# Attention with a local window beside it: score matmuls that ride along, PV in joint bursts, full-width projections

## The chip, the cores and the metric

The kernel runs on one core of a Trainium2 chip. Its engines are TensorE (PE in the profile: matmuls, and PEld, their weight loads), VectorE (DVE), ScalarE (ACT: exp), GpSimd (POOL) and SyncE (SP: it starts transfers). They run side by side, each through its own list of instructions in order, and wait for one another by semaphores. The metric is the device time of one execution in microseconds. Before the change it is 983.29 us (median of 3 runs, 983.21 to 985.47). The execution with a profile spans 983.9 us.

## What is computed

Two attention blocks read the same x (2048 tokens, 512 columns, bf16), and a gate per token mixes them:

```python
def reference(A_x, A_wqkv, A_wo, B_x, B_wqkv, B_wo, gate_w):
    ...
    x = A_x
    g = _sigmoid((x * gate_w).sum(-1, keepdims=True))
    a = _A_ref(x, A_wqkv, A_wo)      # 32 heads of 16, softmax over all 2048 keys
    b = _B_ref(x, B_wqkv, B_wo)      # 32 heads of 16, softmax over 8 keys, 2 apart, backwards
    return g * a + (1 - g) * b
```

Block A is the large one: 32 heads x 2048 x 2048 scores, each of which needs an exp. Block B needs projections on TensorE, and its products and sums run on GpSimd.

## The kernel before

A's work is cut into 32 *periods*: a chunk of 512 queries (`c_`) times a group of 4 heads (`i`). The 4 heads of a group lie on 4 strips of 32 partitions. A *unit* is one head `j` and one block of 128 keys `t`: a score matmul (32 rows x 128 columns of weights, 512 queries) into PSUM, an exp, and a PV matmul into `acc`. A period has 64 units. Most go to ScalarE, in sets of three and two units by turns (PSUM rings `rA` and `rB`); the others go to VectorE, which makes the exp from a polynomial in four operations.

The order of every engine's instructions is fixed when the kernel is built. A small planner runs generators against a model of durations; each `yield (engine, priority, duration, function)` places one step, and the function emits the instructions. `acq` and `rel` take and give back a buffer. Nothing of the planner runs on the chip.

```python
class Plan:
    LAT = 0.08
    ...
P.resource("w", 2)            # two PSUM work banks: projections, transposes, VectorE's scores
P.resource("rA", 1)
P.resource("rB", 1)
P.resource("pTA", 2)
P.resource("pTB", 2)
P.resource("pd", 4)           # results of VectorE's exps
MM = 0.29
```

Projections go through this helper, as four matmuls with 32 columns of weights each, side by side:

```python
def mm_ct(out_, lhsT, rhs, start, stop, **kw):
    for c4 in range(4):
        mm(out_[32 * c4:32 * c4 + 32], lhsT[:, 32 * c4:32 * c4 + 32], rhs, start, stop,
           tile_position=(0, 32 * c4), **kw)

def k_job(i, sc, rel, prio):
    ...
    def pe(c0):
        def f():
            for c in (c0, c0 + 1):
                mm_ct(pk, wkp[:, c, i]..., xT[:, c, sc * QW:(sc + 1) * QW], c == 0, c == DC - 1)
        return f
    yield ("pe", prio, 2 * MM - 0.06, pe(0))
    yield ("pe", prio, 2 * MM - 0.06, pe(2))
```

The same two halves stand in the q projection, in B's projections (`b_proj`, `b_attn`) and, in pairs, in the output projection (`final_job`).

Scores and PV:

```python
def qk_mm(out_, p, t, j):
    c_, i = periods[p]
    mm(out_, kt_all[32 * j:32 * j + 32, i, t * 128:(t + 1) * 128], qt_tiles[p][32 * j:32 * j + 32, :],
       True, True, tile_position=(32 * j, 0))

def pv_step(p, items):
    ...
        for t, j, pt in items:
            pv_left[p] -= 1
            mm(acc[32 * j:32 * j + DH + 1, :], vp_all[:, t, 4 * i + j, :], pt, False, pv_left[p] < 4,
               tile_position=(0, 32 * j))

def pv_job(p, items, res, prio):
    yield ("wait", ev_acc[p])
    ...
    yield ("pe", prio, MM - 0.06 + 0.03 * len(items), pv_step(p, items))

def act_stream():                     # ScalarE's sets
    while front[0] < NP:
        ...
        want = 3 if k % 2 == 0 else 2
        ...                           # units in the order t, j
        yield ("pe", 0, MM - 0.06 + 0.03 * len(units), f)          # f: their scores into the ring
        yield ("spawn", act_tail(k, parts, rname, slot, ring, units))   # exp, then a pv_job

def dve_stream(z):                    # two of these: VectorE's units
    while front[0] < NP - 1 or len(pend[NP - 1]) >= DV_MIN:
        s = yield ("acq", "w", EXP_PRIO)
        ...
        yield ("pe", 1.5, MM - 0.03, lambda: qk_mm(wv_[:], p, t, j))
        ...                           # four VectorE operations, the last into pd
        yield ("spawn", pv_job(p, [(t, j, st["pd"][:])], ("pd", ds), 0.9))
```

So every set's PV is a step of its own, and every VectorE unit has a score step and a PV step of its own. At the end of a period `acc` is copied, transposed (fp32, four matmuls) and divided; after a chunk's last period come the output projections.

Of the kernel before, what the change touches and what calls it, by code (L numbers as in the profile page):

```python
# [47 lines left out]
class Plan:  # L48
# [3 lines left out]
    LAT = 0.08  # L52
# [8 lines left out]

    def resource(self, name, n):
        self.slots[name] = [(0.0, k) for k in range(n)]
        self.reqs[name] = []

# [3 lines left out]
    def advance(self, gen, t, val):  # L69
        while True:  # L70
# [10 lines left out]
            if op == "rel":  # L81
                self.slots[req[1]].append((t, req[2]))
                continue
# [23 lines left out]
            eng, prio, dur, fn = req  # L107
            self.seq += 1
            self.ready[eng].append((prio, self.seq, t, gen, dur, fn))
            return  # L110

    def run(self):
        while True:
            best = None
            for e, lst in self.ready.items():
                if lst:
                    st = max(self.free[e], min(x[2] for x in lst))
                    if best is None or st < best[0]:
                        best = (st, 1, e)
# [9 lines left out]
            if kind == 0:  # L129
                lst = self.reqs[nm]  # L130
                x = min(y for y in lst if y[2] <= st + 1e-9)
                lst.remove(x)
                s = min(y for y in self.slots[nm] if y[0] <= st + 1e-9)
                self.slots[nm].remove(s)
                self.advance(x[3], st, s[1])
            else:
                lst = self.ready[nm]
                x = min((y for y in lst if y[2] <= st + 1e-9), key=lambda y: (y[0], y[1]))
                lst.remove(x)
                x[5]()  # L140
                self.free[nm] = st + x[4]
                self.advance(x[3], st + x[4] + self.LAT, None)


@with_exitstack
def kernel(
# [55 lines left out]

    def mm_ct(out_, lhsT, rhs, start, stop, **kw):
        for c4 in range(4):
            mm(out_[32 * c4:32 * c4 + 32], lhsT[:, 32 * c4:32 * c4 + 32], rhs, start, stop,
               tile_position=(0, 32 * c4), **kw)
# [76 lines left out]
    P.resource("pd", 4)  # L283
    P.resource("prod", 1)
    P.resource("vsh", 1)
    P.resource("ob", 1)
    MM = 0.29
    VP = 0.66
    EXP_PRIO = 60

# [25 lines left out]
    def k_job(i, sc, rel, prio):  # L316
# [3 lines left out]
        s = yield ("acq", "w", prio)  # L320
        pk = wtile(s, [128, QW])

        def pe(c0):
            def f():
                for c in (c0, c0 + 1):
                    mm_ct(pk, wkp[:, c, i].rearrange("p j d -> p (j d)"), xT[:, c, sc * QW:(sc + 1) * QW],
                          c == 0, c == DC - 1)
            return f
        yield ("pe", prio, 2 * MM - 0.06, pe(0))
        yield ("pe", prio, 2 * MM - 0.06, pe(2))  # L330
        kt = kt_all[:, i, sc * QW:(sc + 1) * QW]
        yield ("dve", prio, VP, lambda: V.tensor_scalar(out=kt, in0=pk[:], scalar1=kbias[:, 0:1], scalar2=None,
                                                        op0=ALU.add))
        yield ("rel", "w", s)
# [14 lines left out]
    def v_job(h0, h1, tb, TB, rel, prio):  # L349
# [5 lines left out]
        s = yield ("acq", "w", prio)  # L355
        pv = wtile(s, [128, TB, n])

        def pe(t0, t1):
            def f():
                for tt in range(t0, t1):  # L360
                    for c in range(DC):
                        mm(pv[:, tt, :], xT[:, c, (tb + tt) * 128:(tb + tt + 1) * 128],
                           wv[:, c, h0 * DH:h1 * DH], c == 0, c == DC - 1)
            return f
        step = max(1, TB // 4)
        for t0 in range(0, TB, step):
            yield ("pe", prio, 0.07 * 4 * step, pe(t0, t0 + step))
        yield ("dve", prio, VP, lambda: V.tensor_copy(out=vp_all[:, tb:tb + TB, h0:h1, 0:DH],
                                                      in_=pv[:].rearrange("p t (h d) -> p t h d", d=DH)))
        yield ("rel", "w", s)  # L370
# [6 lines left out]
    def q_job(p, rel, prio):  # L377
# [4 lines left out]
        s = yield ("acq", "w", prio)  # L382
        p1 = wtile(s, [128, QW])

        def pe(c0):
            def f():
                for c in (c0, c0 + 1):
                    mm_ct(p1, wqp[:, c, i].rearrange("p j d -> p (j d)"), xT[:, c, c_ * QW:(c_ + 1) * QW],
                          c == 0, c == DC - 1)
            return f  # L390
        yield ("pe", prio, 2 * MM - 0.06, pe(0))
        yield ("pe", prio, 2 * MM - 0.06, pe(2))
        st = {}

        def absq():
            st["a"] = work.tile([128, QW], BF16, name="absq", tag="absq", bufs=1)
            hi = p1[:].bitcast(I16).rearrange("p (n two) -> p n two", two=2)[:, :, 1]
# [3 lines left out]
        yield ("pe", prio, MM, lambda: mm_ct(p1, selk_all[:, i, :], st["a"][:], False, True,  # L401
                                                skip_group_check=True))

        def evac():
            qt = work.tile([128, QW], BF16, name="qt", tag="qt", bufs=3)
            V.tensor_scalar(out=qt[:], in0=p1[:], scalar1=QSC, scalar2=qbias[:, 0:1], op0=ALU.mult, op1=ALU.add)
            qt_tiles[p] = qt
        yield ("dve", prio, VP, evac)
        yield ("rel", "w", s)
        yield ("set", ev_q[p])  # L410

    def g_job(prio):
# [3 lines left out]
        s = yield ("acq", "w", prio)  # L416
        zp = wtile(s, [128, NT])

        def pe(t0):
            def f():  # L420
                for t in range(t0, t0 + 4):
                    for c in range(DC):
                        mm(zp[:, t:t + 1], xT[:, c, t * 128:(t + 1) * 128], gw[:, c:c + 1], c == 0, c == DC - 1)
            return f
        for t0 in range(0, NT, 4):
            yield ("pe", prio, 0.8, pe(t0))
        e1 = work.tile([128, NT], FP32, name="e1", tag="e1", bufs=1)
        yield ("act", -1, 0.3, lambda: A.activation(out=e1[:], in_=zp[:], func=ACT.Exp, scale=-1.0))
        yield ("rel", "w", s)
# [7 lines left out]
    pend = [deque((t, j) for t in range(NT) for j in range(4)) for _ in range(NP)]  # L437
    front = [0]
    acc_tiles = {}
    pv_left = [64] * NP  # L440
    nset = [0]
    ndve = [0]

# [5 lines left out]
    def pv_step(p, items):  # L449

        c_, i = periods[p]

        def f():
# [6 lines left out]
            for t, j, pt in items:  # L460
                pv_left[p] -= 1
                mm(acc[32 * j:32 * j + DH + 1, :], vp_all[:, t, 4 * i + j, :], pt, False, pv_left[p] < 4,
                   tile_position=(0, 32 * j))
        return f

    def after_pv(p):
        if pv_left[p] == 0:
            return post_job(p)
        return None

    def pv_job(p, items, res, prio):
        i = periods[p][1]
        yield ("wait", ev_acc[p])
        for t, j, _ in items:
            yield ("wait", ev_v[(i, t)])
        yield ("pe", prio, MM - 0.06 + 0.03 * len(items), pv_step(p, items))
        if res is not None:
            yield ("rel", res[0], res[1])
        nx = after_pv(p)
        if nx is not None:  # L480
            yield ("spawn", nx)

    def act_tail(k, parts, rname, rslot, ring, units):
        pname = "pTA" if k % 2 == 0 else "pTB"
        pslot = yield ("acq", pname, k)
        n = len(units)
# [10 lines left out]
        for q_, (p, us) in enumerate(parts):  # L497
            items = [(t, j, pT[:, off + z, :]) for z, (t, j) in enumerate(us)]
            off += len(us)
            last = q_ == len(parts) - 1  # L500
            yield ("spawn", pv_job(p, items, (pname, pslot) if last else None, 1 + 1e-4 * k))

    def act_stream():
        while front[0] < NP:
# [5 lines left out]
            units, parts = [], []  # L510
            p = front[0]
            while want and p < NP:
                us = []
                while want and pend[p]:
                    us.append(pend[p].popleft())
                    want -= 1
# [3 lines left out]
                if not pend[p]:  # L520
# [10 lines left out]
            ring = ps.tile([128, 3 if k % 2 == 0 else 2, QW], FP32, tag=rname, bufs=1, name="ring")  # L531

# [3 lines left out]
            yield ("pe", 0, MM - 0.06 + 0.03 * len(units), f)  # L536
            yield ("spawn", act_tail(k, parts, rname, slot, ring, units))

    DV_MIN = 12

    def dve_pick(t_now):
        p = front[0]
        if p >= NP:
            return None
        if len(pend[p]) >= DV_MIN and ev_q[p].time is not None and ev_q[p].time <= t_now:
            return (p,) + pend[p].pop()
        if p + 1 < NP and len(pend[p + 1]) >= DV_MIN and ev_q[p + 1].time is not None and ev_q[p + 1].time <= t_now:
            return (p + 1,) + pend[p + 1].pop()
        return None

    def dve_stream(z):
        yield ("wait", ev_start[0])
        yield ("delay", 1.0 + 1.5 * z)
        while front[0] < NP - 1 or len(pend[NP - 1]) >= DV_MIN:
            s = yield ("acq", "w", EXP_PRIO)
            t_now = yield ("now",)
            u = dve_pick(t_now)
            if u is None:
                yield ("rel", "w", s)
                yield ("delay", 0.7)  # L560
                continue
            p, t, j = u
            n = ndve[0]
            ndve[0] += 1
            wv_ = wtile(s, [128, QW])
            yield ("pe", 1.5, MM - 0.03, lambda: qk_mm(wv_[:], p, t, j))
            lo = wv_[:].bitcast(U16).rearrange("p (n two) -> p n two", two=2)[:, :, 0]
            ta = work.tile([128, QW], FP32, name="ta", tag="ta", bufs=2)
            pr = 40 + 1e-3 * n
            yield ("dve", pr, VP - 0.05, lambda: V.tensor_scalar(out=ta[:], in0=lo, scalar1=A3, scalar2=None,  # L570
                                                                 op0=ALU.mult))
            yield ("dve", pr, VP - 0.05, lambda: V.scalar_tensor_tensor(out=ta[:], in0=ta[:], scalar=A2, in1=lo,
                                                                        op0=ALU.add, op1=ALU.mult))
            yield ("dve", pr, VP - 0.05, lambda: V.scalar_tensor_tensor(out=ta[:], in0=ta[:], scalar=A1, in1=lo,
                                                                        op0=ALU.add, op1=ALU.mult))
# [403 lines left out]
```

## Time and profile before

| | |
|---|---|
| span of the profiled execution | 983.9 us |
| mean granted TensorE clock | 0.840 |
| TensorE busy, matmuls | 892.3 us, 7296 |
| ScalarE busy | 871.6 us |
| VectorE busy | 677.5 us |
| GpSimd busy | 583.6 us |
| first exp of a set starts, last one ends | 36.46 us, 971.8 us |
| sets of 3, of 2 units, one of 1 | 376, 375, 1 |
| units on VectorE | 169 |

How to read it: nearly all instructions come from one recording line of the kernel (L191), so groups are told apart by the tiles that they write and read. `ring<-qt,kt_all` is a score matmul of a set, `w_...<-qt,kt_all` one for VectorE, `pT<-ring` an exp of a set, `acc<-pT,vp_all` and `acc<-pd,vp_all` are PV. Busy times of matmuls overlap their neighbours', so TensorE's busy share is not its work; the distance from start to start is. The row PEclk gives the clock that TensorE was granted, in tenths, in 40 slices of the span. In the answers by windows, each engine's busy microseconds stand with its number of instructions in brackets, then the clock, the share of the DMA engines, and GB/s.

### The profile page before, as it was taken

Reading aid. Unit: us, or ns where it says so; the run is one execution under the profiler, and the core shown is the slowest. Engines: PE = TensorE matmul, PEld = TensorE weight load, DVE = VectorE, ACT = ScalarE, POOL = GpSimd, SP = SyncE. Lnnn points to the kernel's source line nnn. Section 1 sums busy time; section 2 is a strip of 40 time slices with the busy share of each in tenths; the row PEclk is TensorE's granted clock in tenths of the full one; section 3 lists DMA queues with packets and bytes.
Section 4 is the critical chain, followed back from the end, with each engine's and each line's share of the span. In section 5 each row is a group of like instructions: output and inputs, shape, how many; then the busy total and the mean of one; then the engine's idle time right before and its main releaser. Section 6 shows DMA issues by size and latency. Waiting matters only on the chain.

```text
span 983.9 us, 18122 instructions
## 1 busy us (share of the span) xinstructions
PE 892.3 (91%) x7296; PEld 270.9 (28%) x7296; DVE 677.5 (69%) x1178; ACT 871.6 (89%) x770; POOL 583.6 (59%) x543
## 2 busy tenths in 40 slices
PE   2899999999999988998999989989989989899986
PEld 0333333333232322222223222222223222222221
DVE  3544558576757788875763687888884787987575
ACT  0489999999899998998989998898999988998894
POOL 4000075859989696849786986929974979340000
PEclk8679999999799997798759777796799885976795
DMA  9000103221212103211021411111110201000000
GB/s 249 9 2 1 55 12 98 87 66 25 84 60 79 36 12 97 97 55 51 15 86 36 127 36 51 43 43 44 44 43 12 97 1 44 1 1 1 2 1 22
DMA packets 50021, 47.34 MB, mean 48 GB/s; under 512 B 9984, under 2 KB 47360, under 8 KB 49936
## 3 DMA queue, kind: packets, MB, share of 16 engines
q1 hardware_dynamic: 46240, 41.98, 14.1%
q10 hardware_dynamic: 3696, 4.20, 1.5%
q8 instruction: 57, 0.93, 0.4%
q14 instruction: 28, 0.23, 0.1%
HBM read 37.75 MB, written 6.32 MB: 45 GB/s over the span
## 4 chain that ended last, share of the span: by engine, by line
PE 48%; ACT 24%; DVE 14%; issue 10%; DMA 2%; SPq 0%; ACTq 0%; DVEq 0%
ACT pT L191 24%; PE acc L191 18%; PE ring L191 14%; DVE ta L191 9%; DVE pd L191 3%; DMA xT<-in_A_x_dram 2%; DVE accS L191 1%; ACT lg L191 0%; DVE kt_all L191 0%; DVE lg L191 0%; DVE qt L191 0%; DVE absq L191 0%; PE w_5455 L191 0%; PE w_11876 L191 0%; PE w_6192 L191 0%
## 5 line engine op out<-in xcount | busy, mean ns | idle before, releaser
L191 ACT ACTIVATE pT<-ring 128x1536 bf16<-128x1536 f32 x752 | 867.2, 1275 | 86.4 <-PE ring L191 75.8
L191 PE MATMUL ring<-qt,kt_all 32*128 32x512 bf16 x1879 | 353.4, 436 | 49.2 <-ACT pT L191 43.4
L191 PE MATMUL acc<-pT,vp_all 128*17 128x512 bf16 x1879 | 336.3, 432 | 0.0
L191 POOL TENSOR_TENSOR prod<-prod 128x512 f32<-128x512 f32 (+1 forms) x208 | 240.5, 1170 | 6.3
L191 POOL TENSOR_TENSOR prod<-ksh,qb 128x512 f32<-128x512 bf16 x128 | 144.1, 1157 | 157.1 <-DVE qb L191 114.8
L191 POOL TENSOR_TENSOR prod<-vsh,lg 128x512 f32<-128x512 bf16 x128 | 136.6, 1098 | 117.7 <-issue 114.9
L191 PEld LDWEIGHTS <-kt_all 32*128 32x128 bf16 x2048 | 102.7, 93 | 354.8 <-issue 343.6
L191 PEld LDWEIGHTS <-vp_all 128*17 128x17 bf16 x2048 | 72.4, 89 | 220.9 <-issue 219.4
L191 PE MATMUL acc<-pd,vp_all 128*17 128x512 bf16 x169 | 75.2, 479 | 6.2 <-DVE pd L191 5.4
L191 PEld LDWEIGHTS <-xT 128*32 128x32 bf16 (+1 forms) x1152 | 39.0, 99 | 29.8 <-issue 22.0
L191 DVE COPY accS<-acc 128x512 f32<-128x512 f32 x32 | 22.0, 688 | 14.5 <-PE acc L191 13.7
L191 PEld LDWEIGHTS <-wkp 128*32 128x32 bf16 x512 | 14.4, 103 | 33.8 <-issue 15.4
L191 DVE TENSOR_REDUCE kmax_all<-kt_all 128x1 f32<-128x512 bf16 x32 | 21.8, 684 | 0.9
L191 POOL TENSOR_TENSOR ob<-prod 128x512 f32<-128x512 f32 x16 | 20.3, 1270 | 1.3
L191 POOL TENSOR_TENSOR obb<-ob,prod 128x512 bf16<-128x512 f32 x16 | 20.3, 1270 | 1.3
L191 PEld LDWEIGHTS <-wqp 128*32 128x32 bf16 x512 | 15.9, 107 | 17.7 <-issue 13.8
L191 PE MATMUL acc<-ones_t,z_85 128*32 128x512 bf16 x128 | 15.6, 476 | 2.0 <-DVE accS L191 1.8
L191 POOL TENSOR_TENSOR lg<-prod 128x128 f32<-128x128 f32 x32 | 13.6, 425 | 2.5
L191 PE MATMUL w_136<-xT,wkp 128*32 128x512 bf16 x16 | 2.1, 626 | 11.6 <-DMA xT<-in_A_x_dram 11.6
L191 ACT ACT_TABLE_LOAD x1 | 1.3, 1283 | 12.5 <-DMA xT<-in_A_x_dram 12.5
L191 DVE TENSOR_TENSOR lg<-lg,mx 128x256 f32<-128x256 f32 x16 | 10.9, 680 | 0.2
L191 PEld LDWEIGHTS <-oT 128*32 128x32 bf16 x256 | 8.1, 96 | 6.5 <-issue 2.1
(1286 smaller groups left out, 1127.5 us busy)
## 6 DMA issues: line engine op xcount, KB each, us to landing
ksh<-kv_scr SPq DMA_DIRECT2D x16, 1024.0 KB, 6.2
vsh<-kv_scr SPq DMA_DIRECT2D x16, 1024.0 KB, 5.9
kv_scr<-kvs SPq DMA_DIRECT2D x16, 256.0 KB, 2.3
out_dram<-osb SPq DMA_DIRECT2D x16, 128.0 KB, 1.7
bw<-in_B_wqkv_dram ACTq DMA_DIRECT2D x1, 1536.0 KB, 14.1
wraw<-in_A_wqkv_dram ACTq DMA_DIRECT2D x2, 512.0 KB, 5.8
wv<-in_A_wqkv_dram ACTq DMA_DIRECT2D x1, 512.0 KB, 10.1
bwo<-in_B_wo_dram ACTq DMA_DIRECT2D x1, 512.0 KB, 8.8
```

The source lines that it names most:

```text
L191: return chain_on(self._key, f(*a, **k))
```

## The change

It is meant to give TensorE fewer groups of matmuls for the same work, so that ScalarE gets its scores in time, and to keep TensorE's clock from falling.

- *Riders.* VectorE's units have no stream of their own any more. When a set's two or three scores are placed, a unit of a head whose strip is free in this group may ride along into a work bank (`w`), if a bank and a `pd` buffer are free.
- *PV bursts.* PV of a three-unit set is held until the two-unit set after it is done, and both are issued in one step; finished VectorE units join a burst where their strip has room.
- *Full-width projections.* `mm_ct` is gone; a projection is one matmul of 128 columns of weights per 128 rows of contraction, and its four are one step.
- *Zero-weight matmuls.* If the planner counts less than `WARM` (0.47) of the last 3 us as streaming, a burst gets one more matmul with zero weights, which adds nothing to `acc`.
- *The planner.* New durations (a row `MM` 0.22, a change of group `SW` 0.11); work that isn't scores or PV is placed only when ScalarE has enough sets waiting (`fits`); at most two work banks go to such work; V in smaller pieces and B's tiles start at other times.

The core of the diff:

```diff
-    LAT = 0.08
+    LAT = {"pe": 0.15, "act": 0.08, "dve": 0.08, "pool": 0.08, "sp": 0.08}
+    cap_job = 2
+    refill = 0.56
+    patience = 6.0
 ...
+    def quiet(self, window):
+        while self.streamed and self.streamed[0][0] < self.now - window:
+            self.streamed.popleft()
+        return sum(d - 0.11 for _, d in self.streamed)
 ...
+    def fits(self, x, st):
+        if x[0] < 2 or st - x[7] > self.patience:
+            return True
+        lim = max(self.free["act"], st) + sum(y[4] for y in self.ready["act"]) - self.refill
+        return st + x[4] <= lim or self.free["act"] + 3.0 < st
 ...
-    def mm_ct(out_, lhsT, rhs, start, stop, **kw):
-        for c4 in range(4):
-            mm(out_[32 * c4:32 * c4 + 32], lhsT[:, 32 * c4:32 * c4 + 32], rhs, start, stop,
-               tile_position=(0, 32 * c4), **kw)
 ...
-    MM = 0.29
+    MM = 0.22
+    SW = 0.11
+    WARM = 0.47
 ...
     def k_job(i, sc, rel, prio):
-        yield ("pe", prio, 2 * MM - 0.06, pe(0))
-        yield ("pe", prio, 2 * MM - 0.06, pe(2))
+        def pe(s):
+            w.open(s, [128, QW])
+            for c in range(DC):
+                mm(w.t[:], wkp[:, c, i]..., xT[:, c, sc * QW:(sc + 1) * QW], c == 0, c == DC - 1)
+        yield ("pe", prio, 4 * MM + SW, pe, "w")
 ...
     def pv_job(p, items, res, prio, act=True):
+        if act:
+            act_due[p] -= len(items)
+            if len(items) == 3 and act_due[p] > 0:
+                held_pv[p].append((now, items, res))
+                return
+        def f():
+            ...
+            for h in [h for h in held_pv[p] if h[0] <= now]:
+                todo = list(h[1]) + todo
+            cnt = [sum(1 for x in todo if x[1] == j) for j in range(4)]
+            most = max(cnt)
+            for e in list(pdq[p]):       # finished VectorE units
+                if e[0] <= now and (act_left[p] == 0 or cnt[e[2]] < most) and ...:
+                    todo.append(e[1:4])
+            ...                          # PV of todo, rows by rows
+            if P.quiet(3.0) + MM * max(cnt) < WARM * 3.0 and max(row_left[p]) > 0:
+                mm(acc[32 * j:32 * j + 32, :], z32[:], ones_t[:], False, False, tile_position=(0, 32 * j))
 ...
     def act_stream():
-        yield ("pe", 0, MM - 0.06 + 0.03 * len(units), f)
+        def f():
+            for s_, (p_, t, j) in enumerate(units):
+                qk_mm(ring[:, s_, :], p_, t, j)
+            js = [u[2] for u in units]
+            while len(js) < 4:
+                r = rider(js)
+                if r is None:
+                    break
+                ...
+                qk_mm(wt[:], p_, t, j)
+                P.spawn(dve_unit(p_, t, j, s, ds, wt, ndve[0]), ...)
+        yield ("pe", 0, SW + MM, f)
 ...
-    for z in range(2):
-        P.spawn(dve_stream(z))
-    P.spawn(g_job(20))
+    P.spawn(g_job(4))
 ...
-        P.spawn(b_proj(t, ev_start[min(NP - 1, 1 + 2 * t // 2)] if t else ev_start[1], 25 + 0.1 * t))
-        P.spawn(b_attn(t, ev_start[min(NP - 1, 1 + t)], 25 + 0.1 * t))
+        pr = (9 if t < 2 else 16) + 0.1 * t
+        P.spawn(b_proj(t, ev_start[min(NP - 1, max(1, 2 * t - 3))], pr))
+        P.spawn(b_attn(t, ev_start[min(NP - 1, max(1, 2 * t - 3))], pr))
```

## The prediction

> **What bounds the kernel now.** I read the page first: busy times, the row of granted clock, the chain, the costliest groups.
>
> ```profile
> PE 892.3 (91%) x7296; PEld 270.9 (28%) x7296; DVE 677.5 (69%) x1178; ACT 871.6 (89%) x770; POOL 583.6 (59%) x543
> ...
> PEclk8679999999799997798759777796799885976795
> ...
> ACT pT L191 24%; PE acc L191 18%; PE ring L191 14%; DVE ta L191 9%; DVE pd L191 3%; DMA xT<-in_A_x_dram 2%; DVE accS L191 1%; ACT lg L191 0%; DVE kt_all L191 0%; DVE lg L191 0%; DVE qt L191 0%; DVE absq L191 0%; PE w_5455 L191 0%; PE w_11876 L191 0%; PE w_6192 L191 0%
> ...
> L191 ACT ACTIVATE pT<-ring 128x1536 bf16<-128x1536 f32 x752 | 867.2, 1275 | 86.4 <-PE ring L191 75.8
> ```
>
> ScalarE and TensorE are both near 90%, and 75.8 us of ScalarE's idle time ends with a score matmul (ring). The clock row says when: it is rarely at 9 after the first third. So I asked for the busy times in windows, once over all stretches at half clock from 62 us on and once over all at full clock from 42 us on. First one neighbouring pair, then the two sums.
>
> ```profile
> core 0: us, PE busy (x) PEld busy (x) DVE busy (x) ACT busy (x) POOL busy (x), PEclk, DMA share, GB/s
> 492.26:512.74 20.48, 20.18 (x94) 4.31 (x92) 15.05 (x25) 18.21 (x16) 19.76 (x18) 0.50 0.34 104
> ...
> 512.74:553.70 40.96, 39.34 (x435) 14.19 (x435) 17.08 (x34) 40.35 (x37) 28.77 (x27) 1.00 0.19 58
> ...
> sum 292.26, PE 275.86 PEld 57.00 DVE 210.22 ACT 226.51 POOL 186.92; mean PE 13.14 PEld 2.71 DVE 10.01 ACT 10.79 POOL 8.90
> ...
> sum 651.93, PE 597.17 PEld 205.87 DVE 452.21 ACT 639.99 POOL 385.73; mean PE 28.44 PEld 9.80 DVE 21.53 ACT 30.48 POOL 18.37
> ```
>
> At full clock ScalarE is busy 640 of 652 us (98%): it is the bound. At half clock, 21 stretches and 292 us, it is busy 78% (81% without the tail), while TensorE is at 94% or more: there TensorE is the bound. So the time is ScalarE's work, plus what half clock costs. Next, why the clock falls (windows of 3 us, same columns):
>
> ```profile
> 433.00:436.00 3.00, 2.35 (x17) 0.71 (x16) 2.81 (x6) 3.00 (x3) 3.00 (x4) 1.00 0.55 156
> 436.00:439.00 3.00, 2.47 (x18) 0.75 (x17) 2.82 (x6) 3.00 (x4) 3.00 (x3) 1.00 0.79 255
> 439.00:442.00 3.00, 2.54 (x17) 0.82 (x14) 2.96 (x6) 3.00 (x4) 2.84 (x4) 1.00 0.10 32
> 442.00:445.00 3.00, 2.54 (x15) 0.71 (x14) 3.00 (x6) 3.00 (x3) 3.00 (x3) 0.91 0.00 0
> 445.00:448.00 3.00, 2.57 (x14) 0.44 (x13) 2.08 (x4) 2.09 (x3) 2.92 (x4) 0.50 0.00 0
> ```
>
> Only scores and PV run here, no projection, and after some 12 us of that the clock halves. What a step costs I take from the timeline, full clock at 950 us and half clock at 510 us (start, duration), and ScalarE's pace from a stretch in which it never waited:
>
> ```profile
> 950.12 0.39 PE L191 MATMUL ring<-qt,kt_all 32*128 32x512 bf16 x2
> 950.44 0.60 PE L191 MATMUL acc<-pT,vp_all 128*17 128x512 bf16 x5
> 950.97 0.39 PE L191 MATMUL w_12331<-qt,kt_all 32*128 32x512 bf16 x1
> ...
> 510.34 0.60 PE L191 MATMUL ring<-qt,kt_all 32*128 32x512 bf16 x2
> 510.88 1.02 PE L191 MATMUL acc<-pT,vp_all 128*17 128x512 bf16 x5
> 511.83 1.08 PE L191 MATMUL w_6963<-identf,accS 128*128 128x128 f32 x4
> ...
> 933.83 22.72 ACT L191 ACTIVATE pT<-ring 128x1536 bf16<-128x1536 f32 x20
> ```
>
> Matmuls on different strips of the array run together, so a group costs "rows": the most matmuls that share one strip. A one-row group takes 0.32 us from start to start at full clock, a two-row group 0.53: a row is 0.21 and the change of group 0.11. At half clock they are 0.54 and 0.95: 0.41 to 0.43 and again 0.11. An exp set averages 22.72 / 20 = 1.136 us, a pair (3 and 2 units) 2.27.
>
> **What the Trainium skill says.** "TensorE: Matmul & The Clock Gate", Part 1: the clock is either half or full, by how busy TensorE was in a free-running window of 3413 ns; the trace agrees (0.50 or 1.00 only; stretches such as 13.65 and 20.48 us are multiples of 3.413). Part 3 of that page says matmuls in different strips run together, some 4 ns apart; five PV matmuls in 0.60 us agree. "TensorEngine Tiling", Tiling Modes, Key Properties, says a change of tile shape drains the engine; I read the 0.11 us as that. "TensorE ... Clock Gate", Part 1, "HAM oscillation": gaps between bursts can send the clock back and forth, which is what the windows show.
>
> **The change, part by part.** I counted in the order of instructions of both programs, taking 0.2155 us for a row of 512 columns at full clock (the timeline's 0.21; the Clock Gate page, Part 1, gives 215.7 ns from start to start).
>
> - *Riders.* DVE's score units ride in the free strip of a ScalarE score group. Units for DVE go from 169 to 206, sets from 752 to 737. ScalarE: 15 sets x 1.136 = 17 us less. DVE: 37 x 4 operations at about 0.60 = +89 us, to some 760 us, still under the end.
> - *PV bursts.* PV of a three-unit set waits for the two-unit one. Score and PV rows go from 1740 to 1474, so 266 x 0.2155 = 57 us less TensorE.
> - *Fewer groups.* Changes of tile shape between neighbours go from 1677 to 1204: 473 x 0.11 = 52 us less.
> - *Full-width projections.* Four strips side by side or one full-width matmul are both one row: 608 rows before and after. No stream time is won, only instructions (7296 matmuls to about 5300); a projection now adds a change of shape (in the 1204) and is one block of 4 x 0.21 + 0.11 = 0.97 us, where it was two halves.
> - *Zero-weight matmuls.* 135 against 128: only 7 were placed. They can hardly warm anything.
> - *Head and tail.* First exp at 36.5 us, last end 971.8 of 983.9: 36.5 + 12 = 48.5 us, unchanged.
>
> TensorE at full clock: before 542 us of streams + 1677 x 0.11 = 727; after 485 + 132 = 617. A steady pair at full clock falls to 2 x 0.32 + 0.53 = 1.17 us; at half clock to 2 x 0.54 + 0.95 = 2.03, which now fits into ScalarE's 2.27. Before, it was 4 x 0.54 = 2.16 plus 0.45 DVE units with scores and PV of their own, above 2.27.
>
> The sum. Before: 48.5 + 752 x 1.136 (854) + 8 for the small exps (16 of 0.46 us and one shorter) leaves 73 us lost, 12 of them at full clock, some 61 at half clock. After: 48.5 + 737 x 1.136 (837) + 8 = 893.5, + 13 lost at full clock, + what half clock still costs. That last term is the open one.
>
> It has two factors. How often: fewer rows also means a less busy engine. A bare pair is 4 rows in 2.27 us, 38% streaming, against 46% with DVE units of their own. I gave each set in the two orders ScalarE's measured pace and counted the rows placed between set and set: 33% of the 3.4 us windows stream under 47% in the changed one, 14% before. How dear: without a projection nothing is lost now; a projection at half clock is a block of 4 x 0.43 + 0.11 = 1.8 us, of which the pair's slack (0.24) hides little, so some 1.5 us of exp time. Twelve such blocks would cost 18 us, thirty 45. A block also brings the clock back: before, every stretch ended in a window with a projection or a transpose in it. I take about 16 stretches, fewer than the 21 of before since projections are spread, with one block each: 24 us. Predicted: 893.5 + 13 + 24 = 930 us.
>
> **Rivals.** (1) *The clock stays up*: projections and B's tiles are now spread over the run instead of clumped, and the planner weighs its last 3 us. Then half clock costs under 5 us and the time is about 905. Against it: only 7 zero-weight matmuls, though bare stretches are at 38%. (2) *The clock falls more often*: every bare window drops it, 35 stretches of one and a half blocks, 2.2 us each, 77 us; 893.5 + 13 + 77 is 983, the time of before, and all that riders and bursts won is given back. Half of it, 38 us, makes 945. For it: the 33% against 14%. Against it: the dearest part of the old loss, TensorE too slow in bare stretches, is gone by arithmetic. (3) *DVE becomes the bound*: 760 of 930 us is 82%, and riders hold one of two work banks for four operations, so a projection may wait for a bank with TensorE stopped in order behind it. Before, only 5.4 us of TensorE's idle time ended with a pd; I allow 10 us.
>
> **Range and chances.** 899 (rival 1 and a little less lost) to 964 (57 us at half clock, three quarters of rival 2, or half of it with 3 on top). Faster by over 2% is under 963.6: 0.84. Within 2%: 0.12, rival 2 nearly full. Slower: 0.04, if 2 and 3 both hold in full.
>
> **What would show it.** Right: about 1.136 us per set without waits, 737 sets, ScalarE 98% at full clock and at least 88% at half clock, bare half-clock pairs at ScalarE's pace, its idle time before ring near half of 75.8, head and tail the same. Wrong: a mean clock under 0.8 with ScalarE as idle as before; idle time of TensorE ended by DVE; or ScalarE waiting at full clock.

## The result, and the profile after

The changed kernel takes 948.93 us (median of 4 runs, 937.99 to 952.73), the kernel before 983.25 us: a ratio of 0.961, 95% interval 0.952 to 0.970. Predicted were 930 us and a range of 899 to 964. The ratio leaves out the slowest of the four runs, and the profile is of that one: it spans 951.0 us.

From its page: busy times, the granted clock in 40 slices, the chain of waits, and the exps' group.

```profile
PE 800.1 (84%) x5415; PEld 233.3 (25%) x5415; DVE 762.0 (80%) x1326; ACT 851.9 (90%) x755; POOL 582.7 (61%) x543
...
PEclk9999999979879977778689967768788977876795
...
ACT pT L252 48%; PE w L252 11%; PE ring L252 9%; PE acc L252 7%; DMA xT<-in_A_x_dram 2%; DVE ta L252 2%; DVE pd L252 1%; ACT lg L252 0%; DVE kt_all L252 0%; DVE qt L252 0%; DVE vp_all L252 0%; DVE osb L252 0%; DMA out_dram<-osb 0%; SPq L252 0%; DVE accS L252 0%
...
L252 ACT ACTIVATE pT<-ring 128x1536 bf16<-128x1536 f32 x737 | 847.9, 1289 | 74.9 <-PE w L252 34.3
```

The chain now runs through the exps for 48% of the span (24% before); TensorE's three entries here make 27% (scores and PV alone made 32%, all of TensorE 48%). But the clock row still dips from the first third on, and the idle time in front of the exps fell only from 86.4 to 74.9 us. The windows over all stretches at half clock (first sum) and at full clock (second) say it in numbers:

```profile
sum 302.01, PE 274.29 PEld 55.48 DVE 235.80 ACT 254.12 POOL 163.31; mean PE 11.93 PEld 2.41 DVE 10.25 ACT 11.05 POOL 7.10
...
sum 600.79, PE 497.65 PEld 166.98 DVE 502.40 ACT 584.63 POOL 408.48; mean PE 21.64 PEld 7.26 DVE 21.84 ACT 25.42 POOL 17.76
```

ScalarE is busy 97% at full clock (98% before), and 84% at half clock (78% before), the tail included both times. There is as much half clock as before, some 300 us. What happens in one such stretch is seen in windows of one clock period (3.413 us; busy us and count of PE, PEld, DVE, ACT, POOL, then the clock):

```profile
398.35:401.76 3.41, 2.12 (x20) 0.57 (x15) 3.16 (x6) 3.41 (x5) 3.41 (x4) 1.00 0.01 2
401.76:405.17 3.41, 3.06 (x21) 0.55 (x20) 3.34 (x6) 3.40 (x4) 3.33 (x4) 0.50 0.00 0
...
408.59:412.00 3.41, 3.26 (x18) 0.55 (x15) 3.38 (x6) 3.40 (x4) 3.41 (x4) 0.50 0.00 0
412.00:415.41 3.41, 3.41 (x19) 0.78 (x17) 2.90 (x5) 1.45 (x2) 3.25 (x3) 0.50 0.00 0
```

In the first window only scores and PV run, and the clock falls. In the next ones, at half clock, ScalarE is busy 3.40 of 3.41 us: bare scores and PV cost it nothing now. In the last one it drops to 1.45 us. The timeline shows what ran then:

```profile
411.43 0.61 PE L252 MATMUL ring<-qt,kt_all 32*128 32x512 bf16 x2
411.97 1.89 PE L252 MATMUL w<-xT,wqp 128*128 128x512 bf16 x4
413.79 0.61 PE L252 MATMUL ring<-qt,kt_all 32*128 32x512 bf16 x3
414.33 0.62 PE L252 MATMUL acc<-ones_t,z 128*32 128x512 bf16 x4
414.73 0.94 PE L252 MATMUL acc<-pT,vp_all 128*17 128x512 bf16 x5
...
415.49 1.45 ACT L252 ACTIVATE pT<-ring 128x1536 bf16<-128x1536 f32 x1 [2.04 <-PE acc L252]
```

A full-width projection starts at 411.97 and the next scores only at 413.79, 1.82 us later; ScalarE waits 2.04 us. The projection is not all of it: the scores are done at 414.40, but the wait ends with PV (`PE acc`). A `pT` buffer comes free when PV has read it, and the burst that reads it (414.73) stood behind the projection, the scores and the four matmuls that open the next accumulation. In the window after this one the clock is at full again.

To compare runs I split each span. An exp of three units starts 1.331 us after the one before when nothing waits, one of two units 0.904 us. The work is their sum; whatever lies beyond it from one start to the next is a loss, put down to the clock at the earlier start. Up to the first record of the clock, near 50 us, it counts as half; 1.2 to 5.3 us of the loss at half clock lie before 60 us. At full clock I keep waits over 2.2 us apart. Head and tail are the times before the first and after the last exp. All in us; the last two columns are the stretches at half clock that are not over by 60 us and begin before the last exp ends. One that runs on into the tail is counted whole: 12 us of the 290 are tail, none of e3's 24. Each row is one execution, which can lie some us off the median of its runs.

| run | span | work | head + tail | lost at half clock | lost at full clock, short + long waits | stretches | their us |
|---|---|---|---|---|---|---|---|
| before | 983.9 | 839.9 | 48.6 | 74.3 | 21.0 + 0 | 21 | 290 |
| changed | 951.0 | 823.4 | 47.5 | 59.4 | 16.2 + 4.2 | 23 | 300 |
| e1 no zero rows | 947.0 | 823.4 | 48.6 | 52.4 | 18.2 + 4.3 | 25 | 285 |
| e2 zero rows in parallel | 933.2 | 826.5 | 48.2 | 31.6 | 19.0 + 7.6 | 25 | 157 |
| e4 serial zero rows, some | 929.1 | 824.3 | 46.3 | 27.6 | 20.7 + 9.8 | 19 | 99 |
| e3 serial zero rows, all bursts | 921.6 | 826.5 | 48.2 | 10.2 | 28.8 + 7.6 | 7 | 24 |
| e11 the same, limit 90% | 923.0 | 824.7 | 47.4 | 13.7 | 27.4 + 9.7 | 10 | 44 |
| e5 before, with zero rows | 950.1 | 843.9 | 47.0 | 33.1 | 25.9 + 0 | 10 | 99 |
| e7 projections in strips | 942.5 | 823.4 | 47.8 | 51.8 | 15.3 + 4.2 | 23 | 293 |
| e8 own scores | 950.5 | 824.3 | 48.1 | 41.0 | 20.9 + 16.0 | 22 | 222 |
| e10 own scores, zero rows | 933.0 | 831.0 | 47.0 | 9.7 | 28.0 + 17.1 | 8 | 44 |
| e6 own PV | 998.3 | 828.3 | 47.4 | 90.9 | 18.5 + 13.0 | 38 | 338 |
| e9 own PV, zero rows | 964.4 | 831.0 | 48.0 | 25.2 | 31.9 + 28.0 | 14 | 61 |
| e12 own PV, halved projections | 946.5 | 831.0 | 47.3 | 14.2 | 17.3 + 36.4 | 8 | 38 |

From before to changed: 16.5 us less exp work, 15 us less lost at half clock. That is nearly all of the gain in these two traces.

### The profile page after: what moved, and what is told of

Its sections match the earlier page's. It is cut to its first block, busy times and chain, and to the rows that moved or that the text cites. A ratio compares the mean times of both kernels' runs of the same rounds, so it can differ in the third digit from the quotient of the medians.

```text
span 951.0 us, 14436 instructions
## 1 busy us (share of the span) xinstructions
PE 800.1 (84%) x5415; PEld 233.3 (25%) x5415; DVE 762.0 (80%) x1326; ACT 851.9 (90%) x755; POOL 582.7 (61%) x543
## 4 chain that ended last, share of the span: by engine, by line
ACT 49%; PE 27%; issue 18%; DVE 4%; DMA 2%; SPq 0%; ACTq 0%; DVEq 0%
ACT pT L252 48%; PE w L252 11%; PE ring L252 9%; PE acc L252 7%; DMA xT<-in_A_x_dram 2%; DVE ta L252 2%; DVE pd L252 1%; ACT lg L252 0%; DVE kt_all L252 0%; DVE qt L252 0%; DVE vp_all L252 0%; DVE osb L252 0%; DMA out_dram<-osb 0%; SPq L252 0%; DVE accS L252 0%
## 5 line engine op out<-in xcount | busy, mean ns | idle before, releaser
L252 ACT ACTIVATE pT<-ring 128x1536 bf16<-128x1536 f32 x737 | 847.9, 1289 | 74.9 <-PE w L252 34.3
L252 DVE SCALAR_TENSOR_TENSOR ta<-ta,w 128x512 f32<-128x512 f32 x412 | 278.2, 682 | 6.8
L252 PE MATMUL acc<-pT,vp_all 128*17 128x512 bf16 x1842 | 272.9, 450 | 0.4 <-ACT pT L252 0.2
L252 DVE TENSOR_SCALAR ta<-w 128x512 f32<-128x512 uint16 x206 | 141.4, 687 | 42.2 <-PE w L252 40.0
L252 DVE SCALAR_TENSOR_TENSOR pd<-ta,w 128x512 uint16<-128x512 f32 x206 | 139.8, 680 | 3.1
L252 PE MATMUL w<-qt,kt_all 32*128 32x512 bf16 x206 | 94.0, 458 | 0.0
L252 PEld LDWEIGHTS <-vp_all 128*17 128x17 bf16 x2048 | 46.2, 90 | 113.3 <-issue 111.8
L252 PE MATMUL w<-xT,wkp 128*128 128x512 bf16 x128 | 37.7, 423 | 19.0 <-DMA xT<-in_A_x_dram 17.2
L252 PE MATMUL w<-bw,xT 128*128 128x512 bf16 x192 | 51.4, 392 | 0.5 <-DVE otok L252 0.2
L252 PE MATMUL w<-xT,wqp 128*128 128x512 bf16 x128 | 50.2, 536 | 0.0
L252 PEld LDWEIGHTS <-xT 128*128 128x128 bf16 x512 | 32.7, 103 | 37.0 <-issue 23.8
L252 DVE COPY accS<-acc 128x512 f32<-128x512 f32 x32 | 22.0, 687 | 10.2 <-PE acc L252 10.2
```

What stands on the lines that cost most here:

```text
L252: return chain_on(self._key, f(*a, **k))
```

## The experiments

My theory after the result: the clock falls in every 3.4 us window in which too few rows stream, every projection at half clock makes ScalarE wait, and this is what keeps the gain small. The rivals: extra rows only take TensorE's time, or what counts is the number of matmuls and groups. Ratios are to the kernel before, with 95% intervals.

### Is it the clock? Zero-weight rows, four ways

The change's own zero-weight matmul can do little even where it is placed: it goes to the strip with the most PV left, which mostly has one matmul in a burst where another strip has two. So it mostly runs *beside* the burst's second row and adds no streaming (by the trace 73 of e2's 376 begin a row of their own, and 2 of the change's 7).

**e1**, no such matmul:

```diff
-    WARM = 0.47
+    WARM = 0.0
```

> No zero-weight rows beyond the 128 that open an accumulation; nothing else is changed. Both theories: the 7 rows of the changed kernel did nothing, so 0.96 of the time before, 940 to 955 us, about 300 us at half clock.

Measured: 942.4 us, ratio 0.960 (0.957 to 0.964), 285 us at half clock. The 7 rows did nothing.

**e2**, one in every burst, strip as in the change:

```diff
-    WARM = 0.47
+    WARM = 9.0
```

> One zero-weight matmul in every PV burst (376), in the strip that is furthest behind, which mostly runs beside the burst's own second row: TensorE streams 19 us more, not 81. Theory (the clock falls where a 3.4 us window streams under 45%, and half clock is what the change still loses): such windows fall only from 27% to 18%, so 935 to 948 us and at least 180 us at half clock. Rival A (the clock follows the number of matmuls, not the streamed time): under 100 us at half clock, 915 to 925 us. Rival B (added matmuls only take TensorE's time): over 950 us.

**e3**, the same number in the same bursts, but in a strip that the burst uses most:

```diff
-    WARM = 0.47
+    WARM = 9.0
-                j = max(range(4), key=lambda j_: row_left[p][j_])
+                j = max(range(4), key=lambda j_: (row_left[p][j_] > 0, cnt[j_]))
```

> The same 376 zero-weight matmuls in the same places, each in a strip that the burst uses twice already, so that each adds a row: TensorE streams 79 us more. Theory: windows under 45% fall to 8%, half clock to under 110 us, ScalarE idle 30 us less; it has 3.6 us more work (199 units on VectorE, not 206): 912 to 925 us. Rival A: the same as its neighbour with the rows in parallel. Rival B: 79 us more TensorE makes it slower than the changed kernel, over 955 us.

e2's page, and then e3's: clock, and the group of zero-weight matmuls (both with the 128 that open an accumulation).

```profile
PEclk8599999999989988768999998989898998887895
...
L252 PE MATMUL acc<-ones_t,z 128*32 128x512 bf16 x504 | 165.5, 417 | 1.7 <-DVE accS L252 1.2
```

```profile
PEclk9999999999999999999999999999999999999997
...
L252 PE MATMUL acc<-ones_t,z 128*32 128x512 bf16 x504 | 156.7, 389 | 1.9 <-DVE accS L252 1.6
```

Both have 504 such matmuls and the same lists otherwise. In e2 they lie beside other rows: 935.1 us, 0.952 (0.948 to 0.955), 157 us at half clock. In e3 nearly each is a row of its own (350 of 376 by the trace): 925.6 us, 0.942 (0.939 to 0.945), 24 us at half clock, and the loss at half clock falls from 52 us (e1) to 10. The rival that counts matmuls falls, and so does the one in which added rows only cost: TensorE got 79 us more to stream by the order of instructions (some 75 by the trace's rows) and the kernel became 17 us faster than e1, 0.6 us above the range that I gave. It didn't come for nothing: short waits at full clock rose from 18 to 29 us. e2 came out at the lower end of what I expected, with somewhat less half clock than the 180 us.

**e4**, serial rows only under 62%: the same strip as in e3, with

```diff
-    WARM = 0.47
+    WARM = 0.62
```

> Serial zero-weight rows only where the planner counts under 62% of its last 3 us as streaming: 127 rows, 26 us more streaming, windows under 45% at 15%. Theory: half clock about 180 us, 925 to 938 us, between the changed kernel and the one with a row in every burst. Rival B: 950 to 960 us.

Measured: 930.2 us, 0.947 (0.943 to 0.951), 99 us at half clock, in between as the theory has it, with less half clock than the 180 us that I expected.

**e5**, the kernel before with zero-weight rows and nothing else of the change (the planner counts what streams, and plans 0.22 us for the row):

```diff
+            if len(items) == 3 and pv_left[p] > 8 and P.quiet(3.0) < 0.62 * 3.0:
+                j = items[-1][1]
+                mm(acc[32 * j:32 * j + 32, :], z32[:], ones_t[:], False, False, tile_position=(0, 32 * j))
+                return 0.22
```

> The kernel before, with its own scheduling, groups and projections; alone a serial zero-weight row after a three-unit PV where the planner counts under 62% of its last 3 us as streaming: 138 rows, 27 us more streaming. Windows under 45% fall from 10% to 2.5%; VectorE gets 160 units, not 169, so ScalarE has 4 us more work. Theory: half clock under 120 us (before 290), 925 to 945 us, the clock alone being worth as much as the whole change. Rival (TensorE was simply overloaded, and rows added to it cost): 985 to 1010 us.

```profile
PEclk8679999999999997797999988999999999799977
```

Measured: 949.7 us, 0.961 (0.956 to 0.966): 138 rows of zeros in the old kernel are worth as much as the whole change. Half clock 99 us, the loss there 33 in place of 74. The time is 5 us beyond my range; ScalarE has 4 us more work and loses 5 more at full clock.

### The parts of the change

**e7**, projections in four strips again (`mm_ct` in place of `mm`, for all that fill a bank with 512 columns):

> The changed kernel with its projections as four matmuls of 32 columns of weights side by side again (14 thousand instructions on TensorE's list, not 10.6). Rows are the same, the order is the same. Theory: no difference beyond 1%, 940 to 952 us. Rival (full width is faster, or wakes the clock by using the whole array): over 960 us, or a half-clock time that differs from 300 us by over 60.

```profile
PE 793.6 (84%) x7239; PEld 239.4 (25%) x7239; DVE 761.9 (81%) x1326; ACT 851.2 (90%) x755; POOL 583.4 (62%) x543
```

Measured: 942.9 us, 0.957 (0.953 to 0.961), 293 us at half clock. 1800 more matmuls change nothing that can be told. Full width is neither faster nor does it hold the clock better.

**e8**, VectorE's scores as steps of their own:

```diff
-                while len(js) < 4:
+                while False:
                     r = rider(js)
 ...
+    def dve_stream(z):
+        ...
+        while front[0] < NP - 1 or rem(NP - 1) >= DV_MIN:
+            r = rider([])
+            ...
+            yield ("pe", 1.5, SW + MM, lambda: qk_mm(wt[:], p, t, j))
```

> The changed kernel without riders: a VectorE unit's score is a step of its own again, chosen by the same rule (204 units). The order shows that most such steps still land right beside a score group: 8 us more streams, 13 more changes of group. Theory: within 1% of the changed kernel, 938 to 955 us, possibly less half clock, since windows under 45% go from 27% to 21%. Rival (riders are the gain): 960 us or more.

Measured: 953.0 us, 0.969 (0.966 to 0.973): some 10 us slower than e1 and e7 by the medians, 3.5 by the traces of e1 and e8. It loses 41 us at half clock (e1: 52) but 12 us more in long waits. **e10** adds serial zero-weight rows, so that the clock is out of it:

> VectorE's scores as steps of their own, with a serial zero-weight row in every PV burst. ScalarE has 4.5 us more work than in the run with riders and the same rows (925.6 us). Theory: without riders ScalarE lost 15 us more at full clock and less at half clock; with the clock up only the first is left, so 940 to 950 us. Rival (riders are worth nothing): 928 to 934 us.

Measured: 934.7 us, 0.950 (0.947 to 0.953), 9 us slower than e3. 4.5 us of that are ScalarE's work and 9.5 long waits. Riders are worth about 1%, between what the two theories said.

**e6**, each set's PV at once (without zero rows, to be read beside e1):

```diff
-            if len(items) == 3 and act_due[p] > 0:
+            if False:
                 held_pv[p].append((now, items, res))
```

> The changed kernel without the holding of PV: each set's PV is a group of its own again (no zero-weight rows, to be compared with the run without them). The rows stay nearly as they are (490 us of streams, not 484), the changes of group go from 1206 to 1686, 53 us more TensorE; 195 units on VectorE, so 5 us more ScalarE. Theory (TensorE has room at full clock, and a bare pair at half clock is 2.16 us, under ScalarE's 2.27): 950 to 965 us, of which 5 are ScalarE's. Rival (fewer changes of group are the gain): 980 us or more.

```profile
PEclk8599979799987888868677998657778888887686
...
L252 ACT ACTIVATE pT<-ring 128x1536 bf16<-128x1536 f32 x741 | 850.9, 1257 | 116.8 <-PE ring L252 52.2
```

Measured: 1002.7 us, 1.019 (1.015 to 1.022): 60 us slower than e1, slower than the kernel before, far beyond what I expected and where the rival put it. The rows are nearly as many. By the table, whose two traces are 51 us apart, e6 loses 38 us more than e1 at half clock, at much the same price per stretch (2.4 and 2.1 us), but in 38 stretches in place of 25: the clock comes back sooner, after 8.9 us and not 11.4 on average, and falls again. 9 us more go to long waits and 5 to ScalarE's work. So I held the clock up too, **e9** (zero-weight rows after three-unit PV, serial):

```diff
-    WARM = 0.47
+    WARM = 9.0
 ...
+            if len(items) == 3 and P.quiet(3.0) + MM * max(cnt) < WARM * 3.0 and max(row_left[p]) > 0:
+                j = max(range(4), key=lambda j_: (row_left[p][j_] > 0, cnt[j_]))
```

> PV of each set as a group of its own, and a serial zero-weight row after every three-unit PV (355 rows): 563 us of streams and 1683 changes of group. ScalarE has 4.5 us more work than in the run with held PV and a row in every burst (925.6 us). Theory (the 60 us that own PV groups cost came through the clock, which fell 39 times): windows under 45% are 2%, half clock under 80 us, 930 to 945 us. Rival (the 480 more changes of group delay ScalarE at full clock too): 965 us or more with the clock up.

Measured: 965.5 us, 0.982 (0.978 to 0.985), with only 61 us at half clock. My theory that nearly all of it came through the clock falls: of the 60 us 40 stay against e3, and the time is where the rival put it. By the table 20 of them are long waits at full clock, 15 half clock, 4.5 work and 3 short waits. The longest wait is here (timeline of e9, start and duration):

```profile
99.16 0.39 PE L252 MATMUL ring<-qt,kt_all 32*128 32x512 bf16 x3
...
100.41 1.04 PE L252 MATMUL w<-xT,wkp 128*128 128x512 bf16 x4
...
105.84 4.09 PE L252 MATMUL w<-wv,xT 128*128 128x128 bf16 x64
...
111.75 0.38 PE L252 MATMUL w<-absq,selk_all 128*128 128x512 bf16 x1
...
112.48 0.74 DVE L252 TENSOR_SCALAR qt<-w,qbias 128x512 bf16<-128x512 f32 x1
...
113.59 0.39 PE L252 MATMUL ring<-qt,kt_all 32*128 32x512 bf16 x2
...
114.10 5.80 ACT L252 ACTIVATE pT<-ring 128x1024 bf16<-128x1024 f32 x5 [12.73 <-PE w L252]
```

ScalarE runs out of a head group's units at 99 us, and the next group's k, V and q are only then projected: 12.73 us. A new theory, for the rival says only that more groups delay ScalarE: own PV groups cut TensorE's free time into pieces in which a whole projection (0.97 us) finds no room, so it makes ScalarE wait or is put off until it is too late; held PV leaves one long piece. **e12** cuts the projections instead:

```diff
-        yield ("pe", prio, 4 * MM + SW, pe, "w")
+        yield ("pe", prio, 2 * MM + SW, pe(0), "w")
+        yield ("pe", prio, 2 * MM + SW, pe(2))
```

> Own PV groups and serial zero-weight rows as in the run that took 965.5 us, with every projection cut into two steps of two rows (0.54 us in place of 0.97), each placed by itself; 124 more changes of group, 1807. Theory (own PV groups cut TensorE's free time between sets into pieces under 0.97 us, so that a whole projection makes ScalarE wait; held PV leaves one long piece): 935 to 950 us. Rival (the number of groups itself delays ScalarE): 965 us or more.

Measured: 949.8 us, 0.965 (0.962 to 0.969), just inside what the theory gave, and 16 us faster than e9 with 124 more changes of group. So the number of groups is not what cost those 16 us. Short waits fell from 32 to 17 us and the loss at half clock from 25 to 14: whole projections do make ScalarE wait. That own PV groups are the reason isn't shown: with held PV (e3) the short waits are 29 us, nearly e9's 32, so only the 11 us at half clock fit that part, and halved projections with held PV were not run. The rest of the theory fails: the long waits, where one head group ends and the next isn't projected, went from 28 to 36 us, so a projection's size isn't why it comes late. They are 29 us more than e3's, more than all of the 24 us that are left to it. Why own PV makes the planner place projections so late was not taken apart, and stays open.

**e11**, e3's strip with a limit of 0.90 in place of 9.0:

> The best version so far with its limit at 90% of the last 3 us instead of none: 374 rows, the same share of windows under 45% (8%), but 203 units on VectorE, so 2.2 us less ScalarE work: 920 to 927 us, half clock under 60 us. If the rows cost TensorE's time, no difference shows here.

Measured: 926.3 us, 0.943 (0.940 to 0.947), the same as e3. e3 and e11 beat both kernels; by the ratios e3 is 2% faster than the changed one.

The planner's changes (`fits`, the durations, the other start times) and the step of four projection matmuls in place of two halves were not undone by themselves. Held PV (60 us) and riders (about 10) are worth more than the whole change (34), so the parts overlap or the rest of it costs time; which, these runs don't say.

## Why the prediction was right, and where not

- *The bound* was read rightly: ScalarE at full clock, TensorE at half. The gaps between bursts to which I tied the clock's swings are not there: in the windows before its falls TensorE was never idle for more than 0.85 us before the change and 0.78 after it.
- *ScalarE's work*: 17 us less predicted, 16.5 measured. The 1.136 us per set had some waiting in it (1.117 is the pace without any), in both kernels alike, so the difference held.
- *VectorE*: 760 us predicted (677.5 and 89 are 766), 762.0 measured. Rival 3 didn't come about.
- *Bare pairs at half clock*: 2.03 us, under ScalarE's pace. Right: in the half-clock windows after which the clock stayed down ScalarE was busy 95% on average (88% before).
- *Full width and the 7 zero rows*: no effect predicted; e7 and e1 agree. That such a row runs in parallel and couldn't have helped, I did not see.
- *Head and tail*: 48.5 predicted, 47.5 measured.
- *Lost at full clock*: 13 predicted beside 8 for small exps; 20.4 measured for both.
- *Signs*: two failed. At half clock ScalarE was busy 84%, not 88%, and its idle time before the exps was far from halved: 86.4 us before, 74.9 after, 22.6 and 22.2 of them before the first exp. It no longer bears the name `ring` alone:

```profile
ACT pT L252 <- PE w L252: 34.3, 15, 22.2
ACT pT L252 <- PE ring L252: 29.8, 36, 3.9
...
ACT pT L252 <- PE acc L252: 7.5, 6, 2.0
```

- *Sums of the rivals*: rival 1 comes to 907 to 912 us by its own terms, not 905, and half of rival 2 with 3 on top to 955, not 964. The range's upper end rests on the 57 us alone.
- *The term that was mis-sized: what half clock still costs.* I had 16 stretches at 1.5 us, 24 us, against 61 before, so 37 us less. Measured: 59.4 us, 54.9 of them in 23 stretches at 2.4 us, against 74.3 by the same split: 15 us less (22 in e1). That difference is about the whole distance from 930 to 949. Both factors were too small. The count: I took fewer stretches because projections are spread, though my own count of thin windows (33% against 14%) said more; each return of the clock followed a window with projection or transposes in it, and a later thin window dropped it again. The price: the trace has 86 projection matmuls at half clock, 21 blocks, so one block a stretch as I took it, but such a stretch loses 2.4 us and not 1.5; in the one shown above a single wait is 2.04, with PV behind the projection in it. Transposes and the rows that open an accumulation run there too; how much is theirs I did not measure. The truth lies between my centre and rival 2.
- *Fewer groups*, which come from held PV (480 more without it, e6), I priced at 52 us of TensorE time, and took them to lie beside other work at full clock. e6 shows that holding PV alone is worth 60 us of the time; without it the rest of the change loses to the kernel before. 20 of the 60 go when zero rows hold the clock up (e9); of the 40 left, 20 are late projections of the next head group, and these have no cause yet. The same arithmetic of pairs (2.16 us at half clock, under ScalarE's 2.27) gave 950 to 965 us for e6, at least 38 us too little, so that it came within 2% for the change is in part luck.

## What to carry over

When an engine is not the bound, its load still matters if its clock follows that load: count the rows per clock window in the thinnest stretches, and fill them with rows that add to the stream, not with instructions that run beside others. Before a block of work is made larger, see whether the free time between the bound's steps has a piece of that size: with own PV groups, halves were 16 us better than wholes (with held PV it was not run). And undo each part of a large change by itself: here one part carried 60 us and another none.

## What the runs showed of the hardware

The clock fell without any long idle gap: in the changed kernel the 22 falls between 60 and 900 us followed a window in which rows streamed 32 to 45% of the time (start times of rows times 0.2155 us) and in which TensorE was never idle for more than 0.78 us (0.85 in the kernel before), and after windows with 46% or more it stayed. In the kernel before the falls lie at 39 to 55%, so these numbers give no sharp limit. Rows with zero weights counted as activity (24 us of half clock in e3, 285 in e1); beside another row they did less (157 in e2). In the changed kernel 40 half-clock windows with scores and PV alone, in which rows streamed some 60 to 80% of the time, did not bring it back. All 22 returns followed a window with a projection or transposes in it, but 18 windows with some of them kept half clock; in e3 it returned after one window each time, also without them. So what it takes is not settled.
